# Step 0's triangular inverse through DRAM, decoded weights stored from GpSimd's queue, an earlier plan

## The chip, the cores and the metric

One Trainium2 chip, one of its cores. The metric is the device time of one execution in microseconds (us), lower is better.

## The reference

```python
k_n = k / (norm(k) + 1e-6)                              # B=4, H=8, S=768, D=48
for t in range(S):                                      # delta-rule attention
    y[:, :, t] = q_t @ state
    state += beta_t * outer(k_t, v_t - k_t @ state)
x = y as (B*S, 384)
out = sum_e p[:, e] * (relu(x @ w1[e]) @ w2[e])         # 4 experts, 384 -> 1024 -> 384
return (sigmoid(out @ w_gate) * (out @ w_val)) @ w_out  # 384 -> 1536 -> 384
```

All is fp32. The three gate, value and output matrices of the last layer are handed over as 64-bit numbers.

## The kernel before

The sequence is cut into 12 steps (`c` in the code) of 64 tokens. Within a step the delta rule is a triangular system: with L, the strictly triangular part of K K^T scaled by beta, the inverse X of I+L gives the new values, and the state goes on from step to step. `chain(c)` is that work for one step on TensorE (`ks_task`, `half_task`, `tb_task`, `y_task`, `s_task`). Tiles: `LP` holds L and the masked Q K^T of a step, `Lpp` and `Xpp` hold L and X of two steps in the form in which VectorE (DVE) eliminates, one system on each partition, `XT` and `Ld` hold them as TensorE reads them, `V` the values, `R` the right-hand sides, `YQ` and `KI` the operands of the outputs and of the state. Steps 0 to 3 are inverted in halves of 32 (`r` 0 is steps 0 and 1, `r` 1 is steps 2 and 3), later steps whole. Between the two forms a tile goes out to DRAM and comes back in another order: L by `l_out` (tensor `ls`), L's corner by `l_off` (`lo`), X by `x_out` (`xs`), and back by `l_read`, `off_in` and `x_in`.

Two steps at a time go through the experts (phases `m1`, one for each expert, three in the first pair's first two experts, since step 0 runs expert 0 alone) and the gated layer (phase `m2`). Every fp32 product is three matmuls on parts (`split3`); a weight tile is loaded to `raw` by the SP queue (`w_load`, three buffers), rounded on ScalarE (ACT) to `ws`, and DVE takes the rest. In a phase `emit_a` fills `ph`, ACT and DVE split it to `hhi` and `hlo`, and `emit_b` adds to `acc`.

The 64-bit weights of `m2` are turned into fp32 once, in 36 pieces, during the first pair: `dec_load` (SP queue), `dec_scale` (ACT), `dec_join` (three DVE instructions, two on GpSimd, L240 and L241), `dec_store` (L253, on the SP queue) into the tensor `w_d`, which the `m2` loads read as `raw<-w_d`. The five buffers of loads and four of results lie in `dec_a`, `dec_b`, `Lpp` and `Xpp`.

The order of the program is fixed by a plan. `startup()` does step 0 by hand up to the first rows of expert 0: grams `pg` and `pq`, norms, L of steps 0 and 1 through DRAM, the inverse `inv_ops(0, 2, column)` on DVE, and `chain(0)`. While the inverse runs, `column(t)` transposes its columns on TensorE (`px`, 128 matmuls in all), at the columns `RAW_AT` two grams of steps 3 and 2 (`g_raw`, copied to `LP` by ACT) are put between, and at `WARM_COL` one filler matmul on zeros (`warm`). Four copies then bring `px` to `XT`. After startup `slot()` and `fill()` insert, between the matmuls of the phases, what a model of TensorE's time says is due: `todo` (chains, loads), `back["inv"]` (DVE's instructions of an inverse, between the times in `INV2` for `r` 1) and `back["dec"]` (norms and L of steps 2 and 3 at times 15 to 21, then the decode, from `DEC0` to `DEC1`). Model times are microseconds of matmul work since the first phase began. `l_out`, `p_out`, `x_out`, `x_in`, `off_in` are on GpSimd's queue after startup. `plan_chain` puts the scaling of V (`scale_v`, GpSimd, L540) 6 before the chain and the reading of X and the corner 8 before it.

Of the kernel before, what the change touches and what calls it, by code (L numbers as in the profile page):

```python
# [9 lines left out]
F32 = mybir.dt.float32  # L10
# [8 lines left out]
B, H, S, D = 4, 8, 768, 48  # L19
# [14 lines left out]
READ = 16.0  # L34
SERIAL = 0.12
FLIP, MOVE = 2, 6.0
INV2 = 20.0, 24.0, 84.0
AHEADD, LD, LS = 1.5, 6.0, 6.0
WARM = 11
RAW_AT = (6, 8, 10, 12, 16, 18, 20, 22)  # L40
WARM_COL = 22, 30
DEC0, DEC1 = 16.0, 158.0
CH1, CH2, TR1, TR2 = 78.0, 50.0, 44.0, 16.0

INV = [((0, 1), True), ((2, 3), True)]
# [38 lines left out]
def moe_delta_kernel(  # L84
# [165 lines left out]
    def dec_store(n):  # L250
        stored[0] = n + 1
        dec_at[n] = pe_at[0]
        nc.sync.dma_start(out=w2_d[n // 2, :, (n % 2) * DM : (n % 2 + 1) * DM], in_=dec_views(n)[3])  # L253

    def plan_decode(t0, t1):
        def later(n, wait):
# [198 lines left out]
        for g in range(ng):  # L455
            q[0].dma_start(out=l_view(r)[g * w : (g + 1) * w], in_=ld_t[r].rearrange(form))

    def inv_ops(r, parts=1, after=None):
        X, L = x_view(r), l_view(r)
        ng, n = inv_cut(r)  # L460
        ops = []
        for s in range(n - 1):
            nj, nt = s // ng + 1, n - 1 - s
            if INV[r][1] or s < HC:
                row = L[:, s, s + 1 : n]
            else:
                row = L[:, s - HC, C + s - HC + 1 :]
            now_, box = [], {}
            for k in range(min(parts, nj)):
                col, tgt = X[:, k:nj:parts, s : s + 1], X[:, k:nj:parts, s + 1 :]  # L470
                sh = [P, -(-(nj - k) // parts), nt]

                def first(sh=sh, col=col, row=row, box=box, k=k):
                    if k == 0:
                        box["t"] = ivp.tile([P, 17 * HC], F32, tag="itmp", name="itmp")
                    o = k * 17 * HC // parts
                    box[k] = box["t"][:, o : o + sh[1] * sh[2]].rearrange("p (j t) -> p j t", j=sh[1])
                    vec.tensor_tensor(
                        out=box[k], in0=col.to_broadcast(sh), in1=row.unsqueeze(1).to_broadcast(sh), op=ALU.mult
                    )  # L480

                def second(tgt=tgt, box=box, k=k):
                    vec.tensor_tensor(out=tgt, in0=tgt, in1=box[k], op=ALU.subtract)

                cost = 0.13 + sh[1] * sh[2] / 960.0
                now_.append([(cost, first), (cost, second)])
            ops += [o[0] for o in now_] + [o[1] for o in now_]
            if after:
                ops.append((0.0, lambda s=s: after(s + 1)))
        return ops  # L490

    def xs_tile(r):
# [423 lines left out]
    def plan_chain(c, t, gap):  # L916
        rows = chain(c)
        if c > 1:
            plan(t - 6.0, lambda: scale_v(c))
        if c > 1 and c % 2 == 0:  # L920

            def first():
                while inv_done[0] <= INV_OF[c][0]:
                    back["inv"].pop(0)[2]()
                x_in(c)
                off_in(c)

            plan(t - 8.0, first)
        for r, row in enumerate(rows):
            plan(t + gap * r, lambda row=row: [fn() for fn in row], "pe")  # L930
        t1 = t + gap * len(rows)
        if c % 2 == 0 and c:
            plan(t1 - 2 * gap, lambda: (x_in(c + 1), off_in(c + 1)))
        if c + 1 < NC:
            plan(t + 2 * gap, lambda: (load_v(c + 1), load_ks(c + 1)))
            plan(t1 + 3.0 if c > 1 else 75.0, lambda: load_ys(c + 1))
        return t1
# [31 lines left out]
    def startup():  # L969
# [40 lines left out]
        for c, t in enumerate((KQi, KQ1)):  # L1010
# [4 lines left out]
            q[0] = both  # L1015
            l_out(c)
        l_read(0)
        q[0] = sp
        KQ3 = [t[:112, : 2 * H * C].rearrange("p (a h t) -> p a h t", a=2, h=H) for t in dec_mem[2:4]]
        for i in range(2):  # L1020
# [26 lines left out]
        for _ in range(3):  # L1047
            w_load()
        load_ks(1)
        l_off(1)  # L1050
        k2 = dec_mem[4]
        norm_load(k2, 2)


        px = ph_p.tile([P, HC, 2 * H], F32, tag="ph", name="px")
        later = [lambda hg=hg, i=i, c=c, t=t: g_raw(g_mm(i, hg, t), c, i, hg)
                 for c, t in ((3, KQ3), (2, KQi)) for i in range(2) for hg in range(2)]

        def column(t):
            for bp in range(2):  # L1060
                for a in range(2):
                    o, r = 2 * bp + a, slice(a * HC + bp, (a + 1) * HC, 2)
                    nc.tensor.matmul(
                        out=px[o * HC : (o + 1) * HC, t], lhsT=x_view(0)[0:C, :, t],
                        rhs=ident_sb[0:C, r], start=True, stop=True,
                    )
            if t in RAW_AT:
                later.pop(0)()
            warm(1 if WARM_COL[0] <= t < WARM_COL[1] else 0)

        column(0)
        for _, fn in inv_ops(0, 2, column):
            fn()
        for bp in range(2):
            for a in range(2):
                o, cols = 2 * bp + a, slice(a * HC, (a + 1) * HC)
                src = px[o * HC : (o + 1) * HC].rearrange("p t (i h) -> p i h t", i=2)
                dst = XT[o * HC : (o + 1) * HC, :, :, cols]
                if a:
                    nc.scalar.copy(out=dst, in_=src)  # L1080
                else:
                    vec.tensor_copy(out=dst, in_=src)
        xs = xs_tile(0)
        sp.dma_start(out=xs[C:P], in_=x_view(0)[C:P])
        load_v(1)
        q[0] = Turns(sp, pool_q)
# [22 lines left out]
    with tc.manual_schedule():  # L1109
        pre_lo = xp.tile([P, KT, 2 * STEP], F32R, tag="xlo", name="pre_lo")  # L1110
        dec_tiles()
        dpt, k2 = startup()
        q[1] = nc.sync
        vec_at[0] = 0.0
        plan(0.0, lambda: (gate_probs(dpt), load_p(0)))
        for i in range(2):
            plan(0.0, lambda i=i: s_task(0, i), "pe")
        plan(0.0, lambda: load_ys(1))
        plan(22.0, lambda: nc.gpsimd.memset(bdG, 0.0))
        back["dec"].append((15.0, "dve", lambda: nc.scalar.square(out=k2, in_=k2)))  # L1120
        back["dec"].append((16.0, "dve", lambda: norm_sum(k2, 2, 2)))
        back["dec"].append((17.0, "dve", lambda: norms(2, 4)))
        for c in (2, 3):
            back["dec"].append((16.0 + c, "dve", lambda c=c: (scale_l(c), l_out(c), l_off(c))))
        for c in (2, 3):
            back["dec"].append((18.0 + c, "dve", lambda c=c: (scale_p(c), p_out(c))))
        plan_chain(1, 1.0, 1.9)
        plan_tr(1, 12.0, 1.0)
        plan_inv(1, *INV2)
        plan_decode(DEC0, DEC1)  # L1130
        for k in range(1, NPAIR):
            w = W[k]
            if k > 1:
                r0 = max(M2[0] + 27.0, w - 270.0)
                plan_inv(k, r0, r0 + 22.0, w - CH1 - 14.0)
            if k + 1 < NPAIR:
                g0 = w - (161.0 if k > 1 else 116.0)
                plan_norms(2 * k + 2, g0 - 8.0)
                plan_g(2 * k + 2, g0)
                plan_g(2 * k + 3, g0 + 26.0)  # L1140
            plan_chain(2 * k, w - (CH1 if k > 1 else 84.0), 5.9)
            plan_chain(2 * k + 1, w - (CH2 if k > 1 else 46.0), 5.9)
            plan_tr(2 * k, w - (TR1 if k > 1 else 22.0), 4.0)
            plan_tr(2 * k + 1, w - (TR2 if k > 1 else 8.0), 4.0)
        todo.sort(key=lambda r: (r[0], r[1]))

        T, base = 0.0, 0
        for n, (kind, b, e, s0, ns) in enumerate(PHASES):
            nf = NF1 if kind == "m1" else NF2
            part = unit_us(kind, ns) / (2 if kind == "m1" else 3)  # L1150
            h = {}
            if kind == "m1":
                need = [(2 * b + s0 + s, i) for s in range(ns) for i in range(2)]
                while not all(q in x_done for q in need):
                    todo.pop(0)[3]()
            for u in range(nf):
                now[0] = T = T + part * (1 if kind == "m1" else 2)
                h[u] = emit_a(n, base, u)
                slot()
                if u == 1 and n + 1 < len(PHASES):  # L1160
                    load_p(n + 1)
                if LAG <= u < nf - 1:
                    now[0] = T = T + part
                    emit_b(n, base, [u - LAG], [h.pop(u - LAG)])
                    slot()
            now[0] = T = T + part * (LAG + 1)
            us = sorted(h)
            emit_b(n, base, us, [h[u] for u in us])
            slot()
            base += NG1 if kind == "m1" else NG2  # L1170
# [74 lines left out]
```

## Time and profile before

| | |
|---|---|
| median of three runs | 1541.21 us |
| lowest, highest run | 1533.85, 1541.41 us |
| the profiled execution, its own time | 1541.42 us |
| its span in the trace | 1539.7 us |
| TensorE busy in the span | 1457.7 us, 95% |
| DVE, ACT, GpSimd busy | 1054.2, 586.9, 249.8 us |

The profiled execution is 0.2 us from the median, so a sum made on the trace stands for the median. PE is TensorE's matmuls, PEclk the granted clock as a share of the 2.4 GHz level, so 0.50 is 1.2 GHz. In brackets behind an instruction stands how long its engine was idle before it and what released it.

### The profile page before, as it was taken

Reading aid. Unit: us, or ns where it says so; the run is one execution under the profiler, and the core shown is the slowest. Engines: PE = TensorE matmul, PEld = TensorE weight load, DVE = VectorE, ACT = ScalarE, POOL = GpSimd, SP = SyncE. Lnnn points to the kernel's source line nnn. Section 1 sums busy time; section 2 is a strip of 40 time slices with the busy share of each in tenths; the row PEclk is TensorE's granted clock in tenths of the full one; section 3 lists DMA queues with packets and bytes.
Section 4 is the critical chain, followed back from the end, with each engine's and each line's share of the span. In section 5 each row is a group of like instructions: output and inputs, shape, how many; then the busy total and the mean of one; then the engine's idle time right before and its main releaser. Section 6 shows DMA issues by size and latency. Waiting matters only on the chain.

```text
span 1539.7 us, 25218 instructions
## 1 busy us (share of the span) xinstructions
PE 1457.7 (95%) x9949; PEld 1207.5 (78%) x9949; DVE 1054.2 (68%) x1807; ACT 586.9 (38%) x955; POOL 249.8 (16%) x288
## 2 busy tenths in 40 slices
PE   5899698797899999999999999999999999999998
PEld 4698577685687878888888888878888888888877
DVE  6247698795699957788857788757788754444553
ACT  3225344452434334434333434333433333433343
POOL 3003434573001220001120001220001120001100
PEclk7579899798999999999999999999999999999999
DMA  9135685588544385544395544396533453433331
GB/s 223 48 111 163 213 268 178 173 270 210 159 153 131 115 221 160 147 143 152 114 232 160 147 146 149 111 230 159 151 103 106 130 149 109 131 108 101 93 93 62
DMA packets 93382, 231.72 MB, mean 150 GB/s; under 512 B 19600, under 2 KB 27728, under 8 KB 91232
## 3 DMA queue, kind: packets, MB, share of 16 engines
q1 hardware_dynamic: 81312, 193.40, 42.3%
q0 software_dynamic: 9264, 35.86, 9.0%
q8 instruction: 78, 1.28, 0.4%
q10 hardware_dynamic: 2688, 0.85, 0.2%
q14 instruction: 40, 0.33, 0.1%
HBM read 199.48 MB, written 26.66 MB: 147 GB/s over the span
## 4 chain that ended last, share of the span: by engine, by line
PE 73%; DVE 11%; DMA 7%; issue 5%; ACT 2%; POOL 2%; SPq 0%; ACTq 0%; DVEq 0%; POOLq 0%
PE ph L760 36%; PE acc L797 29%; DVE ws L111 3%; PE pu L358 2%; DMA raw<-w_d 2%; DVE Xpp L111 2%; DVE itmp L111 1%; PE pg L326 1%; DMA xd<-Xpp 1%; DVE hlo L111 1%; DVE dec_b L111 1%; PE ps L621 1%; DMA raw<-in_wp 1%; DMA lo<-LP 1%; PE pg L334 1%
## 5 line engine op out<-in xcount | busy, mean ns | idle before, releaser
L760 PE MATMUL ph<-xhi,ws 128*128 128x512 f32 (+1 forms) x2064 | 635.0, 390 | 9.9 <-ACT sg L774 7.6
L797 PE MATMUL acc<-hhi,ws 128*128 128x512 f32 (+1 forms) x1632 | 500.2, 389 | 15.7 <-ACT hhi L767 10.9
L760 PEld LDWEIGHTS ph<-xhi,ws 128*128 128x128 f32 x2064 | 383.1, 189 | 89.0 <-ACT sg L774 8.4
L760 PE MATMUL ph<-xlo,ws 128*128 128x512 f32 (+1 forms) x1032 | 399.3, 387 | 0.0
L797 PEld LDWEIGHTS acc<-hhi,ws 128*128 128x128 f32 x1632 | 306.7, 191 | 78.1 <-ACT hhi L767 11.7
L111 DVE TENSOR_TENSOR ws<-raw,ws 128x768 fp32r<-128x768 f32 x308 | 297.4, 969 | 61.3 <-ACT ws L191 56.3
L797 PE MATMUL acc<-hlo,ws 128*128 128x512 f32 (+1 forms) x816 | 317.4, 389 | 11.1 <-DVE hlo L111 11.0
L191 ACT CAST ws<-raw 128x768 fp32r<-128x768 f32 x308 | 252.9, 829 | 96.5 <-PE acc L797 60.9
L767 ACT ACTIVATE hhi<-ph 128x512 fp32r<-128x512 f32 (+1 forms) x200 | 116.0, 580 | 411.4 <-PE ph L760 404.8
L760 PEld LDWEIGHTS ph<-xlo,ws 128*128 128x128 f32 x1032 | 195.4, 189 | 40.3 <-DVE xlo L111 1.1
L111 DVE SCALAR_TENSOR_TENSOR hlo<-ph,hhi 128x512 fp32r<-128x512 f32 (+1 forms) x200 | 132.8, 665 | 124.3 <-ACT hhi L767 124.1
L797 PEld LDWEIGHTS acc<-hlo,ws 128*128 128x128 f32 x816 | 155.3, 190 | 46.3 <-DVE hlo L111 15.6
L111 DVE TENSOR_TENSOR itmp<-Xpp,Lpp 128x62 f32<-128x62 f32 (+29 forms) x344 | 165.4, 487 | 12.6 <-DMA Lpp<-ls 7.7
L111 DVE TENSOR_TENSOR Xpp<-Xpp,itmp 128x62 f32<-128x62 f32 (+29 forms) x344 | 165.5, 487 | 6.4
L111 DVE TENSOR_TENSOR gv<-ph,sg 128x512 f32<-128x512 f32 x72 | 49.6, 689 | 94.6 <-PE ph L760 84.6
L838 POOL TENSOR_TENSOR ACC<-ACC,ctmp 128x512 f32<-128x512 f32 (+1 forms) x39 | 50.2, 1296 | 357.7 <-DVE ctmp L111 357.3
L776 ACT CAST hhi<-gv 128x512 fp32r<-128x512 f32 x72 | 44.7, 620 | 161.8 <-DVE gv L111 161.8
L111 DVE TENSOR_TENSOR hlo<-gv,hhi 128x512 fp32r<-128x512 f32 x72 | 52.2, 725 | 49.4 <-ACT hhi L776 49.4
L412 POOL DMA_DIRECT2D ld<-LP x16 | 10.7, 667 | 357.4 <-DVE LP L111 357.4
L774 ACT ACTIVATE sg<-ph 128x512 f32<-128x512 f32 x72 | 42.9, 596 | 59.6 <-PE ph L760 59.4
L111 DVE TENSOR_TENSOR ctmp<-acc,pe 128x512 f32<-128x512 f32 (+1 forms) x57 | 37.3, 658 | 23.2 <-PE acc L797 23.2
L358 PEld LDWEIGHTS pu<-R,XT 64*64 64x64 f32 x1024 | 36.2, 151 | 17.1 <-DVE R L111 9.9
(169 smaller groups left out, 1062.5 us busy)
## 6 DMA issues: line engine op xcount, KB each, us to landing
raw<-in_wp SPq DMA_DIRECT2D x200, 384.0 KB, 3.1
raw<-w_d SPq DMA_DIRECT2D x108, 384.0 KB, 3.8
KQ<-in_kq SPq DMA_DIRECT2D x9, 896.0 KB, 7.6
Lpp<-ld POOLq DMA_DIRECT2D x8, 768.0 KB, 13.7
pe<-p_d SPq DMA_DIRECT2D x23, 256.0 KB, 4.4
dec_a<-in_wp SPq DMA_DIRECT2D x15, 384.0 KB, 4.4
Lpp<-in_wp SPq DMA_DIRECT2D x14, 384.0 KB, 5.3
pd<-LP POOLq DMA_DIRECT2D x10, 512.0 KB, 5.5
```

The source lines that it names most:

```text
L111: return fn(*args, **kw)
L191: nc.scalar.copy(out=w[:, 0], in_=t)
L326: nc.tensor.matmul(out=pg[:, j], lhsT=bdG[:, i, h], rhs=kq_t[i][0:112, :, h], start=True, stop=True)
L334: nc.tensor.matmul(out=pg[to, j], lhsT=kq_t[i][at, 0, h], rhs=kq_t[i][at, :, h], start=True, stop=True)
L358: nc.tensor.matmul(out=out[o : o + C], lhsT=lhsT[o : o + C], rhs=rhs[o : o + C], start=True, stop=True)
L621: nc.tensor.matmul(out=ps[C:112, h], lhsT=KI[0:112, 0, i, h], rhs=rhsA[:, i, h], start=True, stop=True)
L760: nc.tensor.matmul(out=res[q], lhsT=lt, rhs=rt, start=(k == 0 and j == 0), stop=(k == KT - 1 and j == 2))
L767: nc.scalar.activation(out=hh, in_=res[0], func=AF.Relu)
L774: nc.scalar.activation(out=sg, in_=res[0], func=AF.Sigmoid)
L776: nc.scalar.copy(out=hh, in_=gv)
L797: nc.tensor.matmul(out=acc_t[d][:, :w], lhsT=lt, rhs=rt, start=(u == 0 and j == 0), stop=(u == nf - 1 and j == 2),)
L838: (nc.vector if e == NE - 1 else nc.gpsimd).tensor_tensor(out=a, in0=a, in1=t, op=ALU.add)
```

## The change

Step 0's inverse is no longer transposed on TensorE. Its first half is written from `Xpp` to the DRAM tensor `xs` by SP when the inverse has ended, and read back into `XT` by four DMAs (`x_in(0)`, L967 before), two each from the queues of SP and ACT; the other half is written behind them. `px`, its 128 matmuls, the fillers between them and the four copies go. The grams of steps 3 and 2 stand in one row before the inverse's end, and behind them four fp32 matmuls that read `Xpp` (`WARM0`) and so begin with the inverse's end, and ten on zeros (`WARM1`). L's corner of step 1 (`l_off(1)`) is sent right behind `l_read(0)`, on both queues.

After startup: `dec_store` is on GpSimd's queue; norms, L and masked Q K^T of steps 2 and 3 are planned 10 earlier, GpSimd's clearing of `bdG` 11 earlier; `r` 1 reads at 10.5 instead of 20 and is spread over 14 to 76 instead of 24 to 84; the decode ends at 150 instead of 158; `scale_v` is planned 9 before the chain instead of 6.

```diff
-INV2 = 20.0, 24.0, 84.0
+INV2 = 10.5, 14.0, 76.0
...
-RAW_AT = (6, 8, 10, 12, 16, 18, 20, 22)
-WARM_COL = 22, 30
-DEC0, DEC1 = 16.0, 158.0
+WARM0, WARM1 = 4, 10
+DEC0, DEC1 = 16.0, 150.0
...
-        nc.sync.dma_start(out=w2_d[n // 2, :, (n % 2) * DM : (n % 2 + 1) * DM], in_=dec_views(n)[3])
+        nc.gpsimd.dma_start(out=w2_d[n // 2, :, (n % 2) * DM : (n % 2 + 1) * DM], in_=dec_views(n)[3])
...
-            plan(t - 6.0, lambda: scale_v(c))
+            plan(t - 9.0, lambda: scale_v(c))
...
         l_read(0)
+        l_off(1)
         q[0] = sp
...
         load_ks(1)
-        l_off(1)
...
-        px = ph_p.tile([P, HC, 2 * H], F32, tag="ph", name="px")
...
-        column(0)
-        for _, fn in inv_ops(0, 2, column):
-            fn()
...
+        for c, t in ((3, KQ3), (2, KQi)):
+            for i in range(2):
+                for hg in range(2):
+                    g_raw(g_mm(i, hg, t), c, i, hg)
+        for _, fn in inv_ops(0, 2):
+            fn()
...
+        for _ in range(WARM0):
+            nc.tensor.matmul(out=idle, lhsT=Xflat[:, :P], rhs=Xflat[:, : 2 * STEP], start=True, stop=True)
+        warm(WARM1)
         xs = xs_tile(0)
+        sp.dma_start(out=xs[0:C], in_=x_view(0)[0:C])
+        q[0] = both
+        x_in(0)
         sp.dma_start(out=xs[C:P], in_=x_view(0)[C:P])
...
-        plan(22.0, lambda: nc.gpsimd.memset(bdG, 0.0))
-        back["dec"].append((15.0, "dve", lambda: nc.scalar.square(out=k2, in_=k2)))
+        plan(11.0, lambda: nc.gpsimd.memset(bdG, 0.0))
+        back["dec"].append((5.0, "dve", lambda: nc.scalar.square(out=k2, in_=k2)))
...
-            back["dec"].append((16.0 + c, "dve", lambda c=c: (scale_l(c), l_out(c), l_off(c))))
+            back["dec"].append((6.0 + c, "dve", lambda c=c: (scale_l(c), l_out(c), l_off(c))))
...
-            back["dec"].append((18.0 + c, "dve", lambda c=c: (scale_p(c), p_out(c))))
+            back["dec"].append((8.0 + c, "dve", lambda c=c: (scale_p(c), p_out(c))))
```

TensorE in startup, where the inverse ends and `chain(0)` (`pu`) begins, before:

```order
L1063 MATMUL px<-ident_sb,Xpp 32x16 x4
L975 MATMUL acc_129<-pre_lo 128x512
L1063 MATMUL px<-ident_sb,Xpp 32x16 x4
L975 MATMUL acc_129<-pre_lo 128x512
L1063 MATMUL px<-ident_sb,Xpp 32x16 x8
L358 MATMUL pu<-R,XT 64x48 x32
L358 MATMUL pu<-Y_112,Ld 64x48 x16
```

and after:

```order
L333 MATMUL pg<-dec_a 64x128 x16
L333 MATMUL pg<-dec_b 64x128 x16
L333 MATMUL pg<-KQ 64x128 x32
L1059 MATMUL acc_129<-Xpp 128x512 x4
L972 MATMUL acc_129<-pre_lo 128x512 x10
L357 MATMUL pu<-R,XT 64x48 x32
L357 MATMUL pu<-Y_112,Ld 64x48 x16
```

The columns are gone, the grams stand together, and all 14 fillers stand between the inverse's end and the chain.

SP's queue where the decode begins, before (`raw` are the weights of the experts, the other loads those of the decode, `w_d` its stores):

```order
L226 DMA dec_b<-in_wp 128x768
L226 DMA Lpp<-in_wp 128x768
L253 DMA w_d<-dec_b 128x384
L183 DMA raw<-in_wp 128x768 x2
L226 DMA Lpp<-in_wp 128x768
L253 DMA w_d<-Xpp 128x384
```

and after:

```order
L225 DMA dec_b<-in_wp 128x768
L736 DMA pe<-p_d 128x256
L182 DMA raw<-in_wp 128x768
L225 DMA Lpp<-in_wp 128x768
L182 DMA raw<-in_wp 128x768
L225 DMA Lpp<-in_wp 128x768
L182 DMA raw<-in_wp 128x768
```

No store stands ahead of a load on SP any more.

GpSimd ahead of step 2's chain, before:

```order
L429 DMA pd<-LP_117 128x1024
L508 DMA xs<-Xpp 128x1024
L511 DMA XT<-xs 32x16x32 x4
L511 DMA Ld<-lo 32x16x32 x2
L240 TENSOR_TENSOR dec_a<-dec_a 128x384
L241 TENSOR_TENSOR Xpp<-Xpp,dec_a 128x384
L540 TENSOR_TENSOR V<-V,nrm_all 128x384 x2
```

and after:

```order
L428 DMA pd<-LP_117 128x1024
L537 TENSOR_TENSOR V<-V,nrm_all 128x384 x2
L508 DMA XT<-xs 32x16x32 x4
L508 DMA Ld<-lo 32x16x32 x2
L239 TENSOR_TENSOR Lpp<-Lpp 128x384
L240 TENSOR_TENSOR dec_b<-dec_b,Lpp 128x384
L252 DMA w_d<-Xpp 128x384
```

V is scaled ahead of the reads of X, the write `xs` now stands 26 rows ahead of the reads, with eight decode pieces between, and every piece ends with a store.

## Rows read from the trace of the kernel before

**Rows 1.** Windows: length, busy time of each engine, PEclk, DMA share, GB/s.
```profile
0.00:129.00 129.00, 104.06 (x1551) 89.17 (x1552) 57.65 (x187) 41.91 (x84) 16.96 (x27) 0.71 0.48 126
129.00:298.00 169.00, 139.44 (x814) 115.60 (x813) 133.38 (x247) 69.08 (x124) 79.85 (x88) 0.90 0.65 210
298.00:420.00 122.00, 105.60 (x936) 85.18 (x935) 88.28 (x140) 54.23 (x97) 44.42 (x50) 0.96 0.71 203
420.00:1540.00 1120.00, 1108.65 (x6653) 917.60 (x6651) 774.95 (x1234) 421.64 (x652) 108.56 (x123) 1.00 0.48 138
```

**Rows 2.** Timeline of TensorE in startup: start, length, instruction, idle before it.
```profile
1.53 5.06 PE L975 MATMUL acc<-pre_lo 128*128 128x512 f32 x11 [1.53 <-DVE pre_lo L111]
...
42.49 1.97 PE L334 MATMUL pg<-dec_b 48*64 48x128 f32 x16 [10.63 <-ACT LP L379]
...
57.72 0.79 PE L975 MATMUL acc<-pre_lo 128*128 128x512 f32 x1
...
67.94 3.54 PE L358 MATMUL pu<-R,XT 64*64 64x48 f32 x61 [0.89 <-ACT XT L1080]
...
91.28 0.77 PE L760 MATMUL ph<-xhi,ws 128*128 128x256 f32 x2
```

**Rows 3.** Timeline of ACT and of DVE, the end of the inverse.
```profile
41.86 1.07 ACT L379 COPY LP<-pg 128x512 f32<-128x512 f32 x2 [14.76 <-DMA lo<-LP]
...
43.56 0.30 DVE L111 TENSOR_TENSOR Xpp<-Xpp,itmp 128x16 f32<-128x16 f32 x2
```

**Rows 4.** DMA issues (median us to landing), and issue times of L967 in ns.
```profile
xs<-Xpp SPq DMA_DIRECT2D x1, 256.0 KB, 2.9
XT<-xs SPq DMA_DIRECT2D x2, 64.0 KB, 2.6
L967 SPq DMA_DIRECT2D XT<-xs x2: 325/713/1101, 81.2 to 81.6; - x2
```

**Rows 5.** Windows of startup, columns as in rows 1.
```profile
7.50:17.30 9.80, 8.45 (x264) 8.06 (x264) 5.26 (x14) 2.31 (x5) 1.26 (x2) 1.00 0.93 213
...
44.00:66.00 22.00, 21.13 (x262) 15.11 (x258) 0.68 (x1) 3.54 (x7) 0.00 (x0) 0.50 0.12 32
66.00:92.00 26.00, 24.50 (x287) 21.43 (x288) 8.81 (x13) 6.93 (x12) 3.75 (x5) 0.50 0.23 62
```

**Rows 6.** Timeline of TensorE: a chain's first product later, at PEclk 1.00.
```profile
341.83 2.07 PE L358 MATMUL pu<-R,XT 64*64 64x48 f32 x64
```

**Rows 7.** The first long stall: timeline of PE, ACT and SP, SP's waits.
```profile
165.72 1.22 PE L797 MATMUL acc<-hhi,ws 128*128 128x512 f32 x2 [10.86 <-ACT hhi L767]
...
164.34 0.83 ACT L191 CAST ws<-raw 128x768 fp32r<-128x768 f32 x1 [12.52 <-DMA raw<-in_wp]
...
160.59 0.33 SPq L253 DMA_DIRECT2D w_d<-dec_b  x1
...
SPq L253 <- POOL dec_b L241: 27.8, 7, 19.5
```

**Rows 8.** Windows behind the two long stalls: length, PE busy, PEclk, DMA.
```profile
165.00:174.00 9.00, 7.58 (x17) 0.51 0.87 313
275.00:280.00 5.00, 4.83 (x67) 0.50 0.87 274
```

**Rows 9.** The second long stall: timeline of PE and of GpSimd.
```profile
275.17 3.72 PE L358 MATMUL pu<-R,XT 64*64 64x48 f32 x64 [8.69 <-DVE R L111]
...
267.91 2.62 POOL L511 DMA_DIRECT2D XT<-xs  x4 [9.08 <-DMA xs<-Xpp]
...
273.70 1.61 POOL L540 TENSOR_TENSOR V<-V,nrm_all 128x384 f32<-128x384 f32 x2
```

**Rows 10.** DVE's busiest stretch, columns as in rows 1, and GpSimd's DMA issues, ns.
```profile
174.00:260.00 86.00, 78.65 (x470) 66.58 (x469) 81.61 (x160) 43.00 (x78) 36.23 (x37) 0.98 0.68 213
...
L511 POOL DMA_DIRECT2D XT<-xs x8: 648/654/703, 267.9 to 326.8; - x8
```

**Rows 11.** Timeline of TensorE: the longest stall of the decode's tail.
```profile
352.02 1.22 PE L760 MATMUL ph<-xhi,ws 128*128 128x512 f32 x2 [5.85 <-ACT sg L774]
```

More of the change, by code (lines that the diff above doesn't have):

```diff
@@ L456, in l_read, with inv_ops @@
             q[0].dma_start(out=l_view(r)[g * w : (g + 1) * w], in_=ld_t[r].rearrange(form))
-    def inv_ops(r, parts=1, after=None):
+    def inv_ops(r, parts=1):
         X, L = x_view(r), l_view(r)
@@ L487, in inv_ops @@
             ops += [o[0] for o in now_] + [o[1] for o in now_]
-            if after:
-                ops.append((0.0, lambda s=s: after(s + 1)))
         return ops
@@ L1049, in startup @@
         load_ks(1)
-        l_off(1)
         k2 = dec_mem[4]
         norm_load(k2, 2)
-        px = ph_p.tile([P, HC, 2 * H], F32, tag="ph", name="px")
[L1056 to L1069, printed above, removed]
-        column(0)
-        for _, fn in inv_ops(0, 2, column):
-            fn()
[L1074 to L1082, printed above, removed]
+        for c, t in ((3, KQ3), (2, KQi)):
[3 more added lines that the diff above has]
+        for _, fn in inv_ops(0, 2):
+            fn()
+        for _ in range(WARM0):
+            nc.tensor.matmul(out=idle, lhsT=Xflat[:, :P], rhs=Xflat[:, : 2 * STEP], start=True, stop=True)
+        warm(WARM1)
         xs = xs_tile(0)
+        sp.dma_start(out=xs[0:C], in_=x_view(0)[0:C])
+        q[0] = both
+        x_in(0)
         sp.dma_start(out=xs[C:P], in_=x_view(0)[C:P])
@@ L1118, in moe_delta_kernel @@
         plan(0.0, lambda: load_ys(1))
-        plan(22.0, lambda: nc.gpsimd.memset(bdG, 0.0))
-        back["dec"].append((15.0, "dve", lambda: nc.scalar.square(out=k2, in_=k2)))
-        back["dec"].append((16.0, "dve", lambda: norm_sum(k2, 2, 2)))
-        back["dec"].append((17.0, "dve", lambda: norms(2, 4)))
+        plan(11.0, lambda: nc.gpsimd.memset(bdG, 0.0))
+        back["dec"].append((5.0, "dve", lambda: nc.scalar.square(out=k2, in_=k2)))
+        back["dec"].append((6.0, "dve", lambda: norm_sum(k2, 2, 2)))
+        back["dec"].append((7.0, "dve", lambda: norms(2, 4)))
         for c in (2, 3):
-            back["dec"].append((16.0 + c, "dve", lambda c=c: (scale_l(c), l_out(c), l_off(c))))
+            back["dec"].append((6.0 + c, "dve", lambda c=c: (scale_l(c), l_out(c), l_off(c))))
         for c in (2, 3):
-            back["dec"].append((18.0 + c, "dve", lambda c=c: (scale_p(c), p_out(c))))
+            back["dec"].append((8.0 + c, "dve", lambda c=c: (scale_p(c), p_out(c))))
         plan_chain(1, 1.0, 1.9)
```

## The prediction

> **What bounds the kernel now.** I read the windows first [rows 1]. From 420 us on TensorE is busy 1108.65 of 1120 us at the full clock, and nothing of the change reaches there: all that it can give lies in the first 420 us, where TensorE works 349 of 420. The idle time and the half clock there have three places. (1) Startup: the inverse ends at 43.86 [rows 3], but the chain's products `pu` begin in earnest at 67.94, and the first expert's `ph` at 91.28 [rows 2]; all of 44 to 92 is at PEclk 0.50 [rows 5]. (2) Experts of the first pair, 129 to 298: 139.44 busy of 169, PEclk 0.90 [rows 1], with two stalls of 10.86 and 8.69 us [rows 7, 9] and half clock behind each [rows 8]. (3) The decode's tail, 298 to 420: 16.4 us idle, the longest piece 5.85 [rows 11].
>
> **Startup, first piece: from the inverse to `pu`.** Before, the grams of steps 3 and 2 sat between the columns and waited 10.63 us for ACT's copy to LP, which waited 14.76 us for the corner's DMA [rows 2, 3]; so the columns were still being done long after the inverse, and the copies to XT ended only before 67.94. After, this route is a sum: 43.86 + some 0.1, the write to DRAM 2.9 to landing, the issues of two reads on each queue (0.33 to 1.10 each), the last read's landing 2.6 [rows 4]: 46.9, then about 48, then 51. The DMA rings are nearly empty then (share 0.12 in 44 to 66, rows 5), so no longer landings are to be expected. What may be later is TensorE itself: 14 fillers stand ahead of `pu`. The ten on zeros took 0.72 to 0.79 each at half clock [rows 2]. An fp32 filler has no row; eight fp32 products of 128 columns, two at a time, took 1.97 [rows 2], so 128 columns cost 0.49 and 512 some 2.0 at half clock, 1.0 at full (estimates). All at half clock they take 8 + 7.6 = 15.6, to 59.5. If the clock rises behind the second of them: 2 x 2.0 + 2 x 1.0 + 10 x 0.22 = 8.2, to 52 (0.22 for 512 columns at 2.4 GHz). For the clock the nearest rows are the opening's eleven such fillers, 5.06 us in all where 11 x 0.75 would be 8.3 [rows 2]: it rose during them, and the grams after them ran at 1.00 [rows 5]. I take this, 53, with 51 and 59.5 as ends: **-15** (-8.5 to -17). The grams have moved ahead and cost nothing if they end before 43.86: eight groups at 1.97 are 16 us, and they start before 30 if the corner has landed, which is sent 8 us earlier. If they end later, fillers and `pu` are late by as much, up to 5.
>
> **Startup, second piece: the chain at which clock.** From 67.94 to 91.28 are 23.3 us, and TensorE is busy 24.50 of 26 in that stretch, all at 0.50 [rows 5]: it is TensorE's time, not that of the engines between. A chain's first product, 64 records, takes 2.07 at PEclk 1.00 and 3.54 (61 records) here [rows 2, 6]. If the fillers leave the clock at 1.00, the small products can hold it: the grams from 7.5 to 17.3, no larger than these, ran 9.8 us at 1.00 [rows 5]. Then busy 22 becomes 11 to 12, and the hand-overs to ACT and DVE, now less covered, add 2 to 3: 14 instead of 23.3, **-9** (0 to -11).
>
> The Trainium skill, "TensorE: Matmul & The Clock Gate", section "HAM oscillation — how this bites in real kernels", says that an engine which stands idle between pieces while it waits for data drops to the lower clock and starts each piece slow. By it a gap between fillers and `pu` would undo this piece; the trace agrees as far as its idle stretches go (0.50 after the stall of 10.86).
>
> **Experts: the stall at 154.9 to 165.7.** TensorE waits for `hhi`, ACT stands before it in a copy of `raw` that waits 12.52 us for its DMA, and that load was issued at 161, just behind a store that SP held at its head until GpSimd's L241 had ended, waiting 19.5 us [rows 7]. With the stores on GpSimd's queue the load goes out when its buffer is free. Also removed is the half clock behind it: 7.58 busy at 0.51, so 3.8. Together 14.7. Cost on the other side: each store is one DMA issue on GpSimd, 0.65 to 0.70 [rows 10], so 36 x 0.67 = 24 us on an engine that is busy 79.85 of 169 [rows 1]; it lies beside other work, and only if it delays V, ACC or the decode does it count. What else could hold SP there: the decode's own loads wait until GpSimd has read their buffers, and raw loads stand behind them. The plan puts GpSimd's other work (L of steps 2 and 3, `bdG`) 10 earlier, which speaks against it.
>
> **The stall at 266.5 to 275.2.** DVE's R waits for V (L540), which stands on GpSimd behind the reads of X, which wait 9.08 us for the write of X [rows 9]. After, V goes first, and the write is due 8 model units earlier with eight decode pieces between it and the reads, so both waits go: 8.69, and 4.83 at half clock behind it [rows 8], 2.4: 11.1.
>
> **How much of 25.8 stays.** DVE is busy 81.61 of 86 us from 174 to 260 [rows 10] and 133.38 of 169 over all of 129 to 298. Without the stalls these 169 become 143, DVE at 93%; the DVE work is the same, and the inverse `r` 1 and the decode are squeezed by 8 in the plan. So part comes back as small waits for `ws` and `hlo`; I take **-20** (-6 to -26).
>
> **The tail.** The plan ends the decode 8 earlier, which can take away the 5.85 stall and its half clock, or move it, since the decode's rate is DVE's: **-3** (0 to -8).
>
> **Sum.** -15 - 9 - 20 - 3 = -47; 1541.4 - 47 = **1494 us**. Own range of this case: 1479 to 1509.
>
> **Rivals.**
> A, the forecast: 1494, chance 0.52.
> B, DVE takes the experts' gains back: DVE is the limit, the stalls turn into many short waits, and only startup counts with some -5 beside it: 1541.4 - 24 - 5 = 1512. For it speaks the 95% from 174 to 260, against it that in the two stalls DVE stood too. 0.20.
> C, the clock stays at 0.50 in startup, by a gap after the fillers or since they don't lift it: `pu` at 59 and 23.3 us of chain, so startup gives 9, and 1541.4 - 9 - 23 = 1509. For it: 44 to 92 was at 0.50 though TensorE was busy 96% [rows 5]. 0.13.
> D, the change doesn't do what it says: SP waits for GpSimd through the decode's loads instead of the stores, the first stall stays (14.7 of 25.8), C holds too: 1541.4 - 9 - 8 = 1525. 0.08.
> E, slower: GpSimd becomes the limit of the decode. From 129 to 298 it has 79.85 busy; were each of the 36 pieces longer by over 1.8 us (65 us, to 145 in the 143 that remain), the decode would trail GpSimd, `m2`'s loads would wait for `w_d`, and ACT, in order, would stop the experts for decode buffers. At 3 us a piece, 108: the decode's end is 45 us late, more than startup's 24 returns: 1541.4 - 24 + 45 = 1562. Against it: issues from GpSimd took 0.65 to 0.70 beside a DVE that is busy 95% [rows 10]. 0.05. Left over for anything else: 0.02.
>
> The Trainium skill, "SBUF — State Buffer", section "A bandwidth-pool intuition that's wrong (but worth ruling out)", gives this rival its reason: a DMA of GpSimd's queue that takes about 620 ns alone takes about 3100 ns beside a copy on DVE, which locks GpSimd out of the port over which it writes descriptors. By it 36 x 2.5 = 90 us would be added (an estimate from that page), and the time would be near E's. The trace doesn't agree so far: 0.65 to 0.70.
>
> **Chances.** About 0.5% (7.7 us) is what a measurement of this kernel can tell from no change, so faster is below 1533.5. A to C and nearly all of D lie there: 0.91; within 0.5%: 0.04, from D's worse half and the rest; slower: 0.05, E. The range must hold 8 in 10: from A's better part, with the bounds of all pieces (-17 - 11 - 26 - 8 = -62, 1479, and a few more for small waits) to D: 1476 to 1526.
>
> **What would show it.** Right: `pu` begins between 51 and 56, `ph` before 71 with PEclk 1.00 before the fillers end; no wait of SP for GpSimd over 3 us between 100 and 200, no PE stall over 4 us before the end of expert 3; V's L537 starts while XT's reads still wait. Wrong: PEclk 0.50 in the chain (C); GpSimd's issues over 1.5 us, raw loads waiting for L239 (E, D); DVE over 96% with PE idle for `ws` or `hlo` in many pieces (B). What lies behind the first pair should show the same 1108 us of work.

## The result and the profile after

The changed kernel takes 1491.11 us (median of 4 runs, 1488.91 to 1494.02), the kernel before beside it 1537.53 (1531.11 to 1541.41): 0.9703 of it, 95% interval 0.966 to 0.9747. The prediction was 1494, 1476 to 1526. The profiled execution of after took 1491.4, its span is 1489.7, against 1541.42 and 1539.7. The total was right. Of its four terms the two of startup were right; the experts gave 11.4 us less than forecast, the tail 6.6 more, and another 5.2 came from behind the first pair, to which the prediction gave nothing. That these came out near the forecast total is luck.

TensorE in startup, timeline of after (columns as in rows 2), and one window of the chain (as in rows 5):

```profile
33.66 6.09 PE L333 MATMUL pg<-KQ 48*64 48x128 f32 x64 [1.15 <-DMA KQ<-in_kq]
44.84 5.65 PE L1059 MATMUL acc<-Xpp 128*128 128x512 f32 x8 [5.08 <-DVE Xpp L110]
49.92 2.88 PE L972 MATMUL acc<-pre_lo 128*128 128x512 f32 x10
52.73 2.07 PE L357 MATMUL pu<-R,XT 64*64 64x48 f32 x64
...
65.79 0.48 PE L757 MATMUL ph<-xhi,ws 128*128 128x256 f32 x2
...
53.00:66.00 13.00, 13.00 (x284) 11.39 (x280) 6.48 (x10) 5.31 (x10) 3.74 (x5) 1.00 0.38 93
```

`pu` begins at 52.73 where it began at 67.94, `ph` at 65.79 where it began at 91.28 [rows 2], and the chain runs at 1.00 where it ran at 0.50 [rows 5]. The grams are done before the inverse ends, so the fillers wait 5.08 us for it.

The first pair by phases: windows that end near the last matmul of each phase, up to 1.5 us before it (length, busy time of PE, of PE's weight loads, of DVE, ACT and GpSimd, PEclk, DMA, GB/s). Lengths of phases, here and below, are good to about 0.7 us. The four windows of each kernel are the second and third phase together (expert 1, and expert 0 for step 1), expert 2, expert 3, and the gated layer. Before:

```profile
125.50:194.80 69.30, 55.04 (x292) 46.74 (x291) 48.97 (x91) 26.39 (x48) 31.44 (x36) 0.90 0.62 202
194.80:233.20 38.40, 34.88 (x145) 27.78 (x145) 37.69 (x74) 20.60 (x37) 14.78 (x16) 0.96 0.85 266
233.20:293.90 60.70, 48.34 (x320) 39.78 (x320) 45.76 (x83) 22.27 (x40) 33.63 (x37) 0.86 0.61 196
293.90:413.20 119.30, 102.90 (x978) 82.94 (x978) 86.28 (x137) 52.62 (x93) 44.42 (x50) 0.96 0.69 199
```

and after:

```profile
98.90:165.40 66.50, 56.42 (x294) 48.22 (x293) 56.00 (x103) 28.88 (x52) 31.92 (x36) 0.92 0.64 213
165.40:201.10 35.70, 32.79 (x144) 26.41 (x143) 34.36 (x70) 18.01 (x34) 20.04 (x24) 1.00 0.89 288
201.10:258.70 57.60, 47.14 (x321) 39.60 (x321) 44.78 (x71) 24.64 (x45) 42.93 (x49) 0.88 0.71 235
258.70:368.40 109.70, 100.44 (x980) 82.61 (x979) 79.61 (x128) 50.10 (x87) 44.34 (x57) 0.95 0.70 196
```

The first phase ends 26.6 us sooner (125.5 to 98.9), the two behind it bring 2.8, expert 2 brings 2.7, expert 3 3.1, the gated layer 9.6, together 44.8 of the 50.0 by which the span is shorter. The other 5.2 lie behind the first pair, some 3.2 of them in the second pair. Measured to the last matmuls themselves, the experts bring 8.8 for the 8.6 of these windows, and the gated layer 10.0 for 9.6.

The second stall has changed its cause. TensorE, ACT and GpSimd ahead of and in step 2's chain, after:

```profile
235.10 0.28 PE L357 MATMUL pu<-R,XT 64*64 64x48 f32 x2 [2.33 <-DMA XT<-xs]
...
248.95 1.44 PE L325 MATMUL pg<-KQ,bdG 112*128 112x128 f32 x5 [7.54 <-ACT bdG L319]
...
232.05 0.54 ACT L229 ACTIVATE dec_b<-dec_a 128x384 f32<-128x384 f32 x1 [6.36 <-DMA w_d<-dec_b]
...
241.68 0.55 ACT L229 ACTIVATE Xpp<-dec_a 128x384 f32<-128x384 f32 x1 [8.63 <-DMA w_d<-Xpp]
...
224.28 0.58 POOL L252 DMA_DIRECT2D w_d<-dec_b  x1
...
228.10 2.35 POOL L537 TENSOR_TENSOR V<-V,nrm_all 128x384 f32<-128x384 f32 x2
230.41 1.35 POOL L508 DMA_DIRECT2D XT<-xs  x2
...
237.21 0.61 POOL L252 DMA_DIRECT2D w_d<-Xpp  x1
```

V comes at 228.1, ahead of the reads of X, as planned; the products wait 2.33 us for X instead of 8.69 for V [rows 9]. But between one store at 224.28 and the next at 237.21 GpSimd issues the transfers of L, scales V and issues the reads. ACT stands in front of a result buffer whose store has not landed, 6.36 and then 8.63 us, and `bdG`, an operand of the next grams that ACT copies from `KQ`, stands behind it in ACT's order and comes late: 7.54 us of TensorE. SP waits for GpSimd there as well, 11.5 us with a load of the decode, as rival D has it, if not for the first stall.

### The profile page after: what moved, and what is told of

Read it like the earlier page. It is cut to its first block, busy times and chain, and to the rows that moved or that the text cites. A ratio compares the mean times of both kernels' runs of the same rounds, so it can differ in the third digit from the quotient of the medians.

```text
span 1489.7 us, 24733 instructions
## 1 busy us (share of the span) xinstructions
PE 1429.9 (96%) x9703; PEld 1190.2 (80%) x9703; DVE 1055.1 (71%) x1805; ACT 585.5 (39%) x953; POOL 274.3 (18%) x324
## 4 chain that ended last, share of the span: by engine, by line
PE 79%; DVE 10%; DMA 4%; issue 3%; ACT 1%; POOL 1%; SPq 0%; ACTq 0%; DVEq 0%; POOLq 0%
PE ph L757 40%; PE acc L794 31%; DVE Xpp L110 2%; PE pu L357 2%; DVE ws L110 2%; PE pg L325 1%; DVE itmp L110 1%; DMA YQ<-pd 1%; PE pk L547 1%; DVE hlo L110 1%; PE ps L618 1%; PE yt L580 1%; PE yt L581 1%; DMA ls<-LP 1%; DMA Lpp<-ls 1%
## 5 line engine op out<-in xcount | busy, mean ns | idle before, releaser
L110 DVE TENSOR_TENSOR itmp<-Xpp,Lpp 128x62 f32<-128x62 f32 (+29 forms) x344 | 169.1, 498 | 13.7 <-DMA Lpp<-ls 8.5
L773 ACT CAST hhi<-gv 128x512 fp32r<-128x512 f32 x72 | 44.7, 621 | 162.0 <-DVE gv L110 162.0
L110 DVE TENSOR_TENSOR hlo<-gv,hhi 128x512 fp32r<-128x512 f32 x72 | 50.9, 708 | 49.4 <-ACT hhi L773 49.4
L325 PE MATMUL pg<-KQ,bdG 112*128 112x128 f32 x256 | 33.6, 287 | 9.5 <-ACT bdG L319 7.8
```

What stands on the lines that cost most here:

```text
L110: return fn(*args, **kw)
L325: nc.tensor.matmul(out=pg[:, j], lhsT=bdG[:, i, h], rhs=kq_t[i][0:112, :, h], start=True, stop=True)
L773: nc.scalar.copy(out=hh, in_=gv)
```

## The experiments

The ratios are to times of the kernel before that were taken together with each run. Short diffs are against the changed kernel unless said otherwise.

**The startup alone** (plan, stores and V's scaling of the kernel before).

```diff
-INV2 = 10.5, 14.0, 76.0
+INV2 = 20.0, 24.0, 84.0
-DEC0, DEC1 = 16.0, 150.0
+DEC0, DEC1 = 16.0, 158.0
-        nc.gpsimd.dma_start(out=w2_d[n // 2, ...
+        nc.sync.dma_start(out=w2_d[n // 2, ...
-            plan(t - 9.0, lambda: scale_v(c))
+            plan(t - 6.0, lambda: scale_v(c))
... (bdG and the five entries of back["dec"] at their old times)
```

> The changed kernel's startup with the plan, the stores and V's scaling of the kernel before. My theory: the startup is a piece by itself, `ph` begins near 66 us and the first phase ends near 99 as in the changed kernel, and the experts keep their two stalls of about 11 and 9 us: 1537 - 26 = 1511 (1505 to 1519). Rival, DVE as the limit of the first pair: DVE must do the same work in less time, so that part of the 26 is taken back before 414 us: 1518 to 1528. Rival, the plan needs the startup's gain: the stalls grow, over 1528.

1511.08 us, 0.9872 (0.9824 to 0.9921): the first theory. `ph` begins at 66.26, the first phase ends at 99.4, and both stalls are there, the first at 138.36 after 9.66 us, the second at 244.34 after 8.56:

```profile
138.36 1.22 PE L794 MATMUL acc<-hhi,ws 128*128 128x512 f32 x2 [9.66 <-ACT hhi L764]
...
244.34 1.94 PE L357 MATMUL pu<-R,XT 64*64 64x48 f32 x31 [8.56 <-DVE R L110]
```

**Everything but the startup** (the kernel before with the constants and lines above as changed).

> The startup of the kernel before with everything else of the change (stores on GpSimd's queue, earlier plan, V's scaling sooner). Theory that the pieces add: the experts and the first gated layer give 1537 - 24 = 1513, with no wait of SP for GpSimd over 12 us. Rival: the slow startup leaves DVE room in which the plan's earlier work can be done, so that this half gives more by itself than in the changed kernel: 1500 to 1508. Rival: nothing of it counts without the startup: over 1525.

1518.03 us (1505.58 to 1520.13), 0.9888 (0.9833 to 0.9942), 5 us above the first theory and with neither rival. The two halves alone give 1.3% and 1.1%, together 2.4% where the change gives 3.0%; the intervals leave room for a plain sum. The phases of its first pair are those of after: 66.3, 37.7, 57.5 and 108.1 us.

**The stores on SP.**

```diff
-        nc.gpsimd.dma_start(out=w2_d[n // 2, ...
+        nc.sync.dma_start(out=w2_d[n // 2, ...
```

> The changed kernel with the 36 stores of decoded weights back on SP's queue. By the step of my prediction SP holds raw weights behind stores again: a stall of TensorE near 120 to 135 us of some 8 to 11 and half clock behind it, 1491 + 12 = 1503 (1498 to 1508). Rival: the earlier plan alone had already taken that wait away (GpSimd is free when the first store is due), and the stores on GpSimd only brought the 8.6 us for which ACT waited for a store: 1491 or less (1485 to 1494).

1491.62 us, 0.9731 (0.9695 to 0.9768), the same as with the stores on GpSimd: the rival. SP's waits at the stores, 90 to 300 us, are back (total, times, longest), yet ACT waits no more than 3.9 us for a weight:

```profile
SPq L252 <- POOL dec_b L240: 60.7, 13, 14.0
...
ACT ws L190 <- DMA raw<-in_wp: 9.1, 8, 3.9
...
247.18 3.14 PE L325 MATMUL pg<-KQ,bdG 112*128 112x128 f32 x13 [4.92 <-ACT bdG L319]
```

Expert 3 is even shorter than after, 54.4 against 57.6, with 4.92 us for `bdG` instead of 7.54 (last row, TensorE): ACT's waits there, 4.61 and 3.50 us, are no longer put down to a store.

**The stores on GpSimd alone** (the kernel before with that one line).

> The kernel before with the stores of decoded weights on GpSimd's queue and nothing else. If the queue is the remedy of the first stall: 1532 - 12 = 1520 (1515 to 1525), no stall over 4 us near 155 to 166. Rival: GpSimd is as late as before, so that the decode's loads or ACT wait for it instead, and each store adds 0.6 to GpSimd: 1532 (1528 to 1536). Slower rival, by writes of descriptors that wait for DVE: over 1540.

1533.76 us, 0.9982 (0.9961 to 1.0003): no change, the first rival. The trace shows both halves of it: the stall of 10.86 is gone, with 3.62, 1.67 and 2.86 in its place, and the second and third phase take 64.9 instead of 69.3; but expert 3 takes 66.3 instead of 60.7, and at 352 us a stall of 10.72 stands where 5.85 was [rows 11]. ACT's longest wait for a store's landing is 17.3 us (waits, 140 to 300 us):

```profile
ACT dec_b L230 <- DMA w_d<-dec_b: 21.0, 2, 17.3
```

**The old plan times with everything else changed.**

```diff
-INV2 = 10.5, 14.0, 76.0
+INV2 = 20.0, 24.0, 84.0
-DEC0, DEC1 = 16.0, 150.0
+DEC0, DEC1 = 16.0, 158.0
... (bdG and the five entries of back["dec"] at their old times)
```

> The changed kernel with the old plan times (inverse of steps 2 and 3 from 20 over 24 to 84, decode to 158, norms and L of steps 2 and 3 at 15 to 21), but stores on GpSimd's queue and V's scaling at 9. If the stores' queue removes the first stall by itself, no stall over 5 us in the second phase: 1491 + 5 = 1496 (1493 to 1500). Rival, after the run with the stores on SP showed no such stall: the earlier plan is the remedy, and here SP's decode loads or ACT wait for GpSimd, which is late, in the stores' place, a stall of 6 to 11 us: 1503 to 1510.

1505.79 us, 0.9804 (0.9784 to 0.9824): 14.7 above after, as the rival had it, but not where it looked. The second and third phase are the same 66.6; expert 3 takes 61.4, the gated layer 117.1, with a stall for `sg`, the sigmoid of the gate. ACT computes it in order behind pieces of the decode, which waited 3.30, 2.46 and 4.44 us for GpSimd and for a store's landing. The last two rows are GpSimd's and TensorE's at the start of step 2's chain:

```profile
325.50 1.22 PE L757 MATMUL ph<-xhi,ws 128*128 128x512 f32 x2 [9.70 <-ACT sg L771]
...
229.84 0.59 POOL L505 DMA_DIRECT2D xs<-Xpp  x1 [0.61 <-DVE dec_a L110]
...
237.78 0.28 PE L357 MATMUL pu<-R,XT 64*64 64x48 f32 x2 [2.11 <-DMA XT<-xs]
```

Here X is written late, at 229.84, just behind V's scaling at 227.61, and the reads wait 4.24 us for it; still the products wait only 2.11 and then 0.99 us for X. With V first the second stall went without the early write too; the write also landed sooner here, after 4.8 us instead of 9.6.

**The decode planned to 158 again.**

```diff
-DEC0, DEC1 = 16.0, 150.0
+DEC0, DEC1 = 16.0, 158.0
```

> The changed kernel with the decode planned to 158 again, everything else of the plan as changed. If the decode's earlier end is what gave the 10 us of the first gated layer, its stall for `sg` near 310 to 325 is back (6 to 10 us and half clock): 1491 + 8 = 1499 (1496 to 1503). Rival: the earlier inverse and norms gave it by clearing DVE, 1490 to 1494.

1493.18 us, 0.971 (0.9673 to 0.9747), and 109.9 us for the gated layer: the rival. The decode's end in the plan is not what gave the gated layer its 10 us. GpSimd's stores show what changed with it (issue times in ns, first and last start), of the old plan and of this kernel:

```profile
L252 POOL DMA_DIRECT2D w_d<-dec_b x18: 580/582/677, 137.6 to 329.7; - x18
```

```profile
L252 POOL DMA_DIRECT2D w_d<-dec_b x18: 582/582/617, 117.7 to 314.0; - x18
```

With norms, L and inverse of steps 2 and 3 ten earlier the first piece is stored 20 us sooner and the last 16, whatever the planned end. Which of the earlier entries does it, the inverse or what GpSimd has to do before it, was not separated.

**V scaled at 6 before the chain.**

```diff
-            plan(t - 9.0, lambda: scale_v(c))
+            plan(t - 6.0, lambda: scale_v(c))
```

> The changed kernel with V's scaling planned 6 before the chain again, so behind the reads of X on GpSimd. Theory of my prediction: DVE's R waits for V, a stall of TensorE of 4 to 9 us at the start of step 2's chain and some half clock, 1491 + 8 = 1499 (1495 to 1503). Rival: with the write of X sent eight pieces earlier the reads of X no longer wait, so GpSimd reaches V only some 4 us later (six issues at 0.66), and the same time stands in front of the products anyway since they wait for X: 1491 (1488 to 1494).

1494.98 us, 0.9738 (0.9716 to 0.9759). It ends where the first theory's range begins, but the trace is the rival's: R waits for V, yet only 2.55 us of TensorE, about the 2.33 that X costs after, and expert 3 takes 57.9 against 57.6. With the early write of X the stall stays away though V comes last; in the run with the old plan times it stayed away though the write was late and V came first. TensorE waits 9.00 us for `bdG` here.

**No fillers, and fewer.**

```diff
-WARM0, WARM1 = 4, 10
+WARM0, WARM1 = 0, 0
```

> The changed kernel without the 14 filler matmuls between the inverse's end and the chain. My theory: `pu` begins at about 51 us (X is back by then) instead of 52.7, but at half clock, which stays through the chain: 22 to 23 us for the chain instead of 13, `ph` at about 74 instead of 65.8, 1491 + 8 = 1499. Rival: the few fillers that stand between the chain's own products lift the clock soon, `ph` at 66 to 69, 1491 to 1494.

1500.2 us, 0.9781 (0.9739 to 0.9823): the theory. X is back at 50.9, `ph` begins at 74.20, and the chain is at 0.50 all the way (TensorE, and a window):

```profile
50.90 3.51 PE L357 MATMUL pu<-R,XT 64*64 64x48 f32 x61 [0.85 <-DMA XT<-xs]
...
74.20 0.77 PE L757 MATMUL ph<-xhi,ws 128*128 128x256 f32 x2
...
51.00:74.00 23.00, 23.00 (x281) 20.09 (x282) 7.24 (x11) 5.71 (x10) 3.74 (x5) 0.50 0.29 82
```

The chain takes 23.3 us, exactly what it took before. So of startup's 25.5 us some 17 come from the way to `pu` (67.94 to 50.9), and the fillers give 10.2 in the chain (23.3 to 13.1) for 1.8 that they delay it. The 17 are not the route through DRAM alone. From the inverse's end to 65.14 TensorE was in grams for 10.46 us before, in fillers for 6.35 and in columns for 6.29 (these overlap); the change takes the grams and fillers out of the way too. The old route without them was not run: the copies behind the last column took 2.6 us (65.27 to 67.9), so it could have ended near 47 (an estimate from these rows), sooner than the 50.9 of the route through DRAM.

```diff
-WARM0, WARM1 = 4, 10
+WARM0, WARM1 = 4, 3
```

> The changed kernel with three fillers on zeros instead of ten behind the four that read X. In the changed kernel `pu` begins without a wait when the fillers end, 52.7, while X was back at about 51. Expected: `pu` at 51, clock still 1.00 through the chain, 1.5 us less: 1489.5. Rival: the gap of up to 1 us before `pu` costs the clock: `ph` 5 to 9 us later, 1496 to 1500.

1494.73 us, 0.9729 (0.9705 to 0.9753), neither: in the profiled execution the inverse ended later, `pu` began at 53.32 at 1.00 and `ph` at 66.4. The clock is kept, no gain is seen; the 3 us above after lie in phases that the edit doesn't touch.

**The corner sent late** (L's corner of step 1).

```diff
         l_read(0)
-        l_off(1)
...
         load_ks(1)
+        l_off(1)
```

> The changed kernel with L's corner of step 1 sent where it was sent before, behind the loads of KS. The copies to LP then wait for that DMA until about 42 us as in the kernel before, and with the two banks of the grams TensorE waits too: six of the eight groups of grams (1.9 us each at half clock) come behind 42.5, then the fillers, `pu` at 61 to 63 instead of 52.7, 1491 + 9 = 1500 (1497 to 1503). Rival: with less behind it in the rings the corner lands before 32 and nothing is late: 1489 to 1493.

1496.08 us, 0.9735 (0.9698 to 0.9773), half of what the theory had. The corner lands late and six groups of grams are still to be done when the inverse ends, as foreseen:

```profile
43.50 3.68 PE L333 MATMUL pg<-dec_b 48*64 48x128 f32 x32 [13.31 <-ACT LP L378]
46.97 4.61 PE L333 MATMUL pg<-KQ 48*64 48x128 f32 x64
...
57.43 2.07 PE L357 MATMUL pu<-R,XT 64*64 64x48 f32 x64
...
47.00:51.50 4.50, 4.50 (x66) 4.24 (x62) 0.00 (x0) 2.34 (x4) 0.00 (x0) 0.80 0.54 107
...
50.00:51.00 1.00, 1.00 (x24) 1.00 (x22) 0.00 (x0) 0.65 (x2) 0.00 (x0) 1.00 0.90 176
```

But the clock rises during them (0.80 over the window of the last row but one, 1.00 in that of the last, a window's columns as above; the four groups of the last grams took 4.61 us here, 6.09 after), so that the fillers are shorter: `pu` comes 4.7 late, not 9.

**Less work for DVE.**

```diff
-            lambda: ts(out=high, in0=high, scalar1=-(2**31), scalar2=None, op0=ALU.bitwise_and),
-            lambda: stt(out=ti, in0=ti, scalar=3, in1=high, op0=ALU.logical_shift_left, op1=ALU.bitwise_or),
```

> The changed kernel with two of the three DVE instructions of each decoded piece left out (the mask of the high words and the join of the two parts), so the weights of the gated layer are other numbers; 72 DVE instructions, some 0.35 to 1.1 us each, 40 us of DVE's time in the first pair. If DVE is what took back the first stall's 14.7 us, the second and third phase become shorter, 66 to 57 to 60, and the fourth, 1491 - 12 = 1479 (1473 to 1484). Rival: those phases wait for the order of GpSimd, ACT and the transfers, not for DVE's load: 1487 to 1493.

1480.62 us, 0.9631 (0.959 to 0.9673): the theory's time, by other phases than it named. Its windows, of an execution of 1476.27, the fastest of the four:

```profile
99.00:162.70 63.70, 54.72 (x292) 46.96 (x291) 53.11 (x93) 29.43 (x54) 38.90 (x43) 0.95 0.68 236
162.70:195.00 32.30, 32.30 (x146) 26.78 (x145) 26.61 (x46) 16.53 (x30) 20.61 (x26) 1.00 0.86 281
195.00:255.90 60.90, 46.35 (x321) 39.30 (x320) 35.46 (x61) 29.21 (x54) 43.49 (x52) 0.89 0.77 260
255.90:352.50 96.60, 96.59 (x978) 79.77 (x978) 60.83 (x100) 47.03 (x79) 32.78 (x45) 1.00 0.71 200
```

Expert 2 and the gated layer now keep TensorE busy without a gap (32.30 of 32.30, 96.59 of 96.60): there DVE's load, with the order that the plan gives it, was the limit, or the time that each piece takes on its way, which the edit shortens as well. The second and third phase are only 2.8 us shorter, but this does not clear DVE: its busy time there fell by 2.9 only (56.00 to 53.11). Eight pieces are stored in these phases instead of six, and the 16 products of `ws` took 20.0 us instead of 15.2. Six of them took 1.58 to 1.99 us; each of the six began within 0.1 us of an instruction of GpSimd's, the others took 0.94 to 1.20 (GpSimd, and DVE beside it and alone):

```profile
121.76 0.82 POOL L239 TENSOR_TENSOR dec_b<-dec_b 128x384 f32<-128x384 f32 x1 [2.35 <-issue]
...
121.81 1.59 DVE L110 TENSOR_TENSOR ws<-raw,ws 128x768 fp32r<-128x768 f32 x1
...
147.50 0.94 DVE L110 TENSOR_TENSOR ws<-raw,ws 128x768 fp32r<-128x768 f32 x1
```

Expert 3 is longer.

**The stores on SP and the next inverse's transfers later.**

```diff
-        nc.gpsimd.dma_start(out=w2_d[n // 2, ...
+        nc.sync.dma_start(out=w2_d[n // 2, ...
-                r0 = max(M2[0] + 27.0, w - 270.0)
+                r0 = max(M2[0] + 40.0, w - 270.0)
```

> The changed kernel with the stores on SP again and the transfers of the next inverse (2.5 MB to Xpp and Lpp) planned 13 later, so behind the 0.5 MB of masked Q K^T that step 3's outputs wait for. The stall of 5 to 7 us for YQ in the first gated layer and its half clock go: 1491.5 - 7 = 1484 (1482 to 1487). Rival: another of the transfers of that stretch (the weights, V, KS) takes the wait over: 1489 to 1493.

1499.4 us, 0.9756 (0.9717 to 0.9795): both theories fail. The edit does what it was for, the gated layer takes 103.1 instead of 109.4 us, but the inverse of steps 4 and 5 is late in its turn, and the second pair takes 246.0 instead of 233.1, with this stall:

```profile
514.00 0.42 PE L357 MATMUL pu<-R,XT 64*64 64x48 f32 x2 [8.02 <-DMA XT<-xd]
```

Of all these kernels only the one that leaves work out was faster than the changed one.

## Why the prediction was right, and where it was not

**Startup, -15 and -9: right, -25.5.** `pu` at 52.73 for 53, `ph` at 65.79 for 67. The sum for X ran as worked out: inverse's end 44.7 (0.8 later than before), reads issued at 47.6, X there at 50.9 without fillers. The clock rose during the fillers and the small products kept it; without them it stayed at 0.50. The four fp32 fillers took 5.65 us where the sum has 6.0, and the ten on zeros 2.88 where it has 2.2; from the inverse's end to `pu` they took 8.0 for 8.2. The corner's place was worth 4.7, which the prediction had as a condition.

**Experts, -20: too much, -8.6** (2.8, 2.7 and 3.1 by the windows above; still within the term's own -6 to -26). The step that failed is "How much of 25.8 stays". It lets a quarter of 25.8 come back; two thirds did. Both stalls went, but the phases hardly shortened.

In the second and third phase TensorE's idle time fell from 14.3 to 10.1 us only, though the stall of 10.86 went: other waits fill its time, 3.03 for `ws` and 3.90 and 2.58 for `hlo`, all from DVE, as this one after:

```profile
137.59 0.79 PE L794 MATMUL acc<-hlo,ws 128*128 128x512 f32 x1 [3.90 <-DVE hlo L110]
```

The variants take about as long there with the first stall (startup alone, 65.4) and without it: 66.6 with stores on GpSimd and the old plan, 66.5 and 65.6 with the new plan and stores on either queue, 69 with fewer or no fillers. These are the short waits of rival B, but its sign, DVE over 96%, did not show: DVE was busy 84% there (56.00 of 66.50). The prediction also took DVE's work as the same; the earlier plan moved some of it into these phases, where DVE spent 19.4 us in the products of the inverse, against 6.9 before. How far DVE holds them stays open, since the run with less work for DVE hardly lightened it there.

In expert 3 the 8.69 for V gave way to 2.33 for X and 7.54 for `bdG`, so that the sign "no PE stall over 4 us before the end of expert 3" failed as well.

**The stores' queue: named as the remedy of the first stall, worth nothing in time.** The run with that line alone measured 0.9982 of the kernel before, with 1 inside its interval, and the run without it 0.9731, where the change has 0.9703 with an interval that overlaps. The wait moved from SP, where it held the weights, to ACT, where it holds what stands behind it in order: rival E in small. As for its price, issues took 0.54 to 0.71 us and landings 2.2 to 7.7 (the rows of one of the two buffers):

```profile
L252 POOL DMA_DIRECT2D w_d<-Xpp x18: 539/581/692, 125.0 to 315.4; - x18
...
DMA to landing us min/median/max: 2.2/3.2/7.7
```

The long issues that rival E had as its reason, 3.1 us each, did not show; that GpSimd works in order did.

**V: its place was not needed.** The prediction took V's place and the earlier write of X together. The early write does it with V last (V scaled at 6, a wait of 2.55). V's place did it with a late write too (the old plan times, 2.11 and 0.99 for X), but that write landed in half the time of before, so what V's place is worth without it was not separated.

**The tail, -3: too little, -9.6.** The prediction tied it to the decode's planned end; that end has no effect. With the earlier norms, L and inverse of steps 2 and 3 the decode begins 20 us sooner, and the stall for `sg` with its half clock went (1.19 us left). A longer wait for the masked Q K^T took some of it back, 5.25 us where 1.38 stood before:

```profile
338.27 0.44 PE L580 MATMUL yt<-YQ,rhsA 112*64 112x64 f32 x2 [5.25 <-DMA YQ<-pd]
```

This term makes up for more than half of what the experts did not give.

**Behind the first pair, 0: -5.2.** The second pair took 235.2 and 236.6 us in the kernel before and with the startup alone, the two that have both the old plan and the stores on SP, and 232.0 to 233.8 in the other kernels (the last one above aside), two of which have the old plan with stores on GpSimd. No experiment settles the cause.

## What to carry to other kernels

A stall that is removed gives back at most the time until the next limit of that stretch: compare the lengths of the phases in several variants, not the stalls, before a stall's length is put into a sum. Ask of each moved DMA which engine now waits for its landing and what stands behind that wait in order: a wait taken from a load queue and given to a computing engine can cost the same. Fillers on an engine that would idle pay where a long train of small products follows them (10.2 us for 1.8), and work that starts sooner in the plan may be worth more than another queue: here the earlier plan times brought 14.7 us and the stores' queue nothing. When one edit moves several things on the same way, as the one to `pu` does, run them apart before the route gets the credit.

## What the runs showed of the hardware

DVE slows down beside GpSimd's arithmetic. The same product, 128 by 112, in the second phase, with the engines beside it; before, while GpSimd cleared `bdG`:

```profile
157.39 0.28 DVE L111 TENSOR_TENSOR itmp<-Xpp,Lpp 128x112 f32<-128x112 f32 x1
...
156.77 1.80 POOL L1119 MEMSET bdG<- 112x2048 f32 x1
```

and after, while GpSimd multiplied a decoded piece:

```profile
114.50 0.91 DVE L110 TENSOR_TENSOR itmp<-Xpp,Lpp 128x112 f32<-128x112 f32 x1
115.44 1.07 DVE L110 TENSOR_TENSOR Xpp<-Xpp,itmp 128x112 f32<-128x112 f32 x1
...
114.44 0.83 POOL L239 TENSOR_TENSOR dec_a<-dec_a 128x384 f32<-128x384 f32 x1
115.35 1.03 POOL L240 TENSOR_TENSOR dec_b<-dec_b,dec_a 128x384 f32<-128x384 f32 x1
```

0.28 us became 0.91, and the next instruction ends about when GpSimd's second does (116.51 and 116.38). The Trainium skill, "SBUF — State Buffer", section "Who interferes with whom", says that a DVE instruction with two inputs in SBUF contends with a GpSimd instruction that reads SBUF, not with one that only writes; both rows agree. Each of the 36 pieces has two such instructions, so the first pair's DVE time has this in it, before and after, as the `ws` products of the run with less work for DVE show too (0.94 us, and 1.58 to 1.99 beside GpSimd). The prediction did not price it, and it may be part of what holds the second and third phase, which no run tried.

The clock rose from 0.50 to 1.00 during the grams of steps 3 and 2 in one row when the corner came late (the windows above). During the same grams with columns and single fillers between them, in the kernel before, it stayed at 0.50 for 22 us, with TensorE busy 96% [rows 5], and in the chain without fillers it stayed there with TensorE busy 23.00 of 23.00 us. So a stretch's busy share alone does not tell whether the clock rises in it: rival C took 0.50 at a share of 96% as a sign that the fillers might not lift it, and they did.
